# A fixed order on every engine for routed attention with a squared-ReLU feed-forward, its weights rounded as a pipeline

## The chip, the cores and the metric

The kernel runs on one core of a Trainium2 chip. A core has engines that run side by side, each with its own queue of instructions that it works off in order: TensorE (PE, matrix products; PEld is its loading of weights), VectorE (DVE), ScalarE (ACT), GpSimd (POOL) and SyncE (SP), which here issues the transfers between device memory and the core's memories. An engine waits for another by semaphores. SBUF is the working memory of 128 partitions; PSUM holds what TensorE writes, in eight banks. The metric is the device time of one execution in microseconds (us).

## The reference

Attention in which a query sees only the keys of its own cluster, and on its output a feed-forward block with a squared ReLU. All tensors are float32 (the weights come as float64 and are rounded on the chip).

```python
# q, k, v: (4, 8, 768, 64); centroids: (8, 16, 64)
q_assign = np.argmax(np.einsum('bhsd,hcd->bhsc', q_n, c_n), axis=-1)
k_assign = np.argmax(np.einsum('bhsd,hcd->bhsc', k_n, c_n), axis=-1)
mask = q_assign[:, :, :, None] == k_assign[:, :, None, :]
scores = np.where(mask, scale * np.matmul(q, k.transpose(0, 1, 3, 2)), -1e9)
attn = np.exp(scores - np.max(scores, axis=-1, keepdims=True))
x = np.matmul(attn / (np.sum(attn, axis=-1, keepdims=True) + 1e-9), v)
# x to (3072, 512); w_in: (512, 2048), w_out: (2048, 512)
r = np.maximum(x @ w_in, 0.0)
out = (r * r) @ w_out
```

## The kernel before

*Units.* Heads are worked on in pairs; a pair is two heads of one batch (`HP` = 4 pairs a batch, `NG` = 16 in all). A unit is one pair, one half `h` of the queries (384 of 768) and two of the six chunks of 128 keys. There are 96: first the four pairs of batch 0 with half 0 (units 0 to 11), then the same with half 1 (12 to 23), then each later pair with both halves. For each chunk, `scores` (L321) multiplies keys and queries of both heads into the PSUM tile `sc` and ACT takes the exponential into a tile `ex` (L337). For batch 0 the mask is a second product of one-hot cluster numbers on top of the scores (L332); for later pairs DVE multiplies `ex` by a comparison of cluster numbers (L339). POOL adds the six chunks up into `acc` (L347, L351). Two units later (`LAG`) `times_v` (L357) multiplies the exponentials by v into `av`. When a half is complete, `finish` sums `acc` over its partitions with a matmul into `sm` (L372), takes the reciprocal (L376), checks it (L378) and writes the quotient to `xT` (L382).

*Preparing a pair.* `prep` makes seven items for a pair: three `turn` (transposes of q and k into `pt`, copied to `qkT` by ACT, the second by DVE), `logits` (product with the centroids, copy `lgs`), `route` (transposes into `lt`, then four or five DVE steps that find the cluster, L258 to L279), and twice `turn_onehot` (batch 0) or `spread` (later pairs: two times three products `pb`, each three copied to `qid` by ACT). `load_qk(pair + 1)` is issued when a pair's transposes are done.

*Feed-forward.* `ffn(b, h)` is a generator of 112 steps for one half of a batch: 64 for `ph` (L395, four a tile, then ACT's ReLU L402 and DVE's square L403 into one of 16 `gT`), then 48 for `po` (L408), whose three results go by ACT to `osb` and out. `fill_steps` puts these steps among the units, evenly over those to come; what is left at the end runs alone.

*Banks.* Two banks each for `sc` and `av`; two (`ps_f`, by `bank`) for all else: `pt`, `lg`, `lt`, `po` of the one-hots, `pb`, `sm`, `ph`, `po`.

*Weights.* The 32 blocks of 128 x 512 float64 are read as pairs of words (`lo`, `hi`) and turned to float32 by `round_weights` (L118): DVE cuts out the exponent (L126), ACT shifts its bias (L129), DVE bounds it and sets the sign (L130, L134) and cuts out the mantissa (L139), ACT scales both halves (L142, L143), POOL adds them and multiplies (L144, L145, into `w_in` or `w_out`). Raw blocks have two buffers (`wstage`), `w_power` has one (`wtmp`). In the loop, 4/3 blocks are rounded in each of the first 12 units, two in each later one, until all 32 are done.

*Order.* The loop is traced unit by unit, and a scheduler then decides in which order the instructions stand on each engine; so TensorE's items of several steps can be taken apart and mixed.

Of the kernel before, what the change touches and what calls it, by code (L numbers as in the profile page):

```python
# [17 lines left out]
P = 128  # L18
# [5 lines left out]
def kernel(  # L24
# [27 lines left out]
    loads = ctx.enter_context(tc.tile_pool(name="loads", bufs=3))  # L52
# [8 lines left out]
    xtp = ctx.enter_context(tc.tile_pool(name="xtp", bufs=3))  # L61
    gtp = ctx.enter_context(tc.tile_pool(name="gtp", bufs=FT))
    outp = ctx.enter_context(tc.tile_pool(name="outp", bufs=1))
    wstage = ctx.enter_context(tc.tile_pool(name="wstage", bufs=2))
    wtmp = ctx.enter_context(tc.tile_pool(name="wtmp", bufs=1))
# [5 lines left out]
    def bank(name, shape):  # L71
        return ps_f.tile(shape, F32, name=name, tag="f")

# [38 lines left out]
    raw_w = {}  # L112

    def load_weights(i):
        raw_w[i] = wstage.tile([P, NW, 2], U32, name="w_raw")
        nc.sync.dma_start(raw_w[i], weights[i][1])

    def round_weights(i):  # L118
        dst = weights[i][0]
        w = raw_w.pop(i)  # L120
        lo, hi = w[:, :, 0], w[:, :, 1]
        lo_f, hi_f = lo.bitcast(F32), hi.bitcast(F32)
        power = wtmp.tile([P, NW], U32, name="w_power")
        power_f = power.bitcast(F32)

        nc.vector.tensor_scalar(  # L126
            out=power, in0=hi, scalar1=0x7FF00000, scalar2=None, op0=ALU.bitwise_and
        )
        nc.scalar.activation(out=power_f, in_=power, func=ACT.Relu, bias=rebias, scale=1.0)  # L129
        nc.vector.tensor_scalar(  # L130
            out=power, in0=power_f, scalar1=float(255 << 20), scalar2=8.0,
            op0=ALU.min, op1=ALU.mult,
        )
        nc.vector.scalar_tensor_tensor(  # L134
            out=power, in0=hi, scalar=0x80000000, in1=power,
            op0=ALU.bitwise_and, op1=ALU.bitwise_or,
        )

        nc.vector.tensor_scalar(  # L139
            out=hi, in0=hi, scalar1=0x000FFFFF, scalar2=None, op0=ALU.bitwise_and  # L140
        )
        nc.scalar.activation(out=hi_f, in_=hi, func=ACT.Copy, bias=1.0, scale=2.0 ** -20)  # L142
        nc.scalar.mul(out=lo_f, in_=lo, mul=2.0 ** -52)  # L143
        nc.gpsimd.tensor_tensor(out=hi_f, in0=hi_f, in1=lo_f, op=ALU.add)  # L144
        nc.gpsimd.tensor_tensor(out=dst, in0=hi_f, in1=power_f, op=ALU.mult)  # L145
# [5 lines left out]
    load_v(0)  # L151
# [11 lines left out]
    rebias = const.tile([P, 1], F32, name="rebias")  # L163
    nc.vector.memset(rebias, -float((1023 - 127) << 20))
# [10 lines left out]
    def centroids_norm():  # L175
# [6 lines left out]
        nc.scalar.sqrt(nrm, ss)  # L182
        for _ in range(2):
# [37 lines left out]
    def turn(pair, part):  # L221
# [7 lines left out]
        if part == 1:  # L229
            nc.vector.tensor_copy(out=dst, in_=pt)  # L230
        else:
            nc.scalar.copy(out=dst, in_=pt)
        if part == 2:
            raw.pop(pair)
            load_qk(pair + 1)
# [3 lines left out]
    def logits(pair):  # L239
# [8 lines left out]
        nc.scalar.copy(out=lgs[pair], in_=lg)  # L248

    def route(pair):  # L250
        lt = bank("lt", [P, NB, P])
        src = lgs.pop(pair)
        for i in range(NB):
            nc.tensor.transpose(out=lt[:, i], in_=src[:, i * P : (i + 1) * P], identity=ident)
        n = NB * P // C
# [8 lines left out]
        nc.vector.tensor_tensor(  # L264
# [16 lines left out]
    def turn_onehot(pair, which):  # L281
# [9 lines left out]
        if which == 0:  # L291
            nc.scalar.copy(out=dst, in_=src)
        else:
            nc.vector.tensor_scalar(
                out=dst, in0=src, scalar1=BIG, scalar2=-BIG, op0=ALU.mult, op1=ALU.add
            )

    def spread(pair, e):
        src, dst = qid[pair]
        for g in range(2):  # L300
# [6 lines left out]
            nc.scalar.copy(out=dst[:, g, e], in_=pb.rearrange("p i n -> p (i n)"))  # L307

# [12 lines left out]
    def scores(pair, h, c):  # L321
# [16 lines left out]
        for e in range(0 if pair < HP else 2):  # L338
            nc.vector.scalar_tensor_tensor(  # L339
                out=t[:, e], in0=qid[pair][1][:, h, e],  # L340
                scalar=ids[pair][:, c % NB, 2 + c // NB, e : e + 1], in1=t[:, e],
                op0=ALU.is_equal, op1=ALU.mult,
            )
        ex[pair, h, c] = t
        if c == 1:
            acc[pair, h] = accp.tile([P, 2, TB], F32, name="acc")
            nc.gpsimd.tensor_tensor(  # L347
                out=acc[pair, h], in0=ex[pair, h, 0], in1=t, op=ALU.add
            )
        elif c > 1:  # L350
            nc.gpsimd.tensor_tensor(out=acc[pair, h], in0=acc[pair, h], in1=t, op=ALU.add)  # L351

    def times_v(pair, h, c):
# [7 lines left out]
        if c > 0:  # L361
            ex.pop((pair, h, c))
            ex.pop((pair, h, 0), None)

    def finish(pair, h):
        b, hp = divmod(pair, HP)
        if hp == 0:
            xT[b, h] = xtp.tile([P, KT, TB], F32, name="xT")
        total = acc.pop((pair, h))
        sm = bank("sm", [P, TB])  # L370
        for e in range(2):
# [3 lines left out]
        rb = rbp.tile([P, TB], F32, name="rb")  # L375
        nc.vector.reciprocal(out=rb, in_=sm)  # L376
        ok = once.tile([P, TB], BF16, name="ok")
        nc.vector.scalar_tensor_tensor(  # L378
            out=ok, in0=rb, scalar=2.0 ** -100, in1=rb, op0=ALU.is_ge, op1=ALU.is_gt,
            accum_out=good[:, 2 * pair + h : 2 * pair + h + 1],  # L380
        )
        nc.vector.scalar_tensor_tensor(  # L382
            out=xT[b, h][:, hp], in0=av.pop((pair, h)), scalar=UP, in1=rb,
            op0=ALU.mult, op1=ALU.mult,
        )
# [4 lines left out]
    def ffn(b, h):  # L390
        gT = []
        for f in range(FT):
            ph = bank("ph", [P, TB])
            for kk in range(KT):
# [4 lines left out]
                if kk < KT - 1:  # L399
                    yield  # L400
            gT.append(gtp.tile([P, TB], F32, name="gT"))
            nc.scalar.activation(out=gT[f], in_=ph, func=ACT.Relu)  # L402
            nc.vector.tensor_tensor(out=gT[f], in0=gT[f], in1=gT[f], op=ALU.mult)  # L403
            yield
        for i in range(NB):
            po = bank("po", [P, DM])
            for f in range(FT):
# [4 lines left out]
                if f < FT - 1:  # L412
                    yield
# [3 lines left out]
            yield  # L417
# [9 lines left out]
    LAG = 2  # L427
    per_half = FT * KT + NB * FT
    fill = []
    left = [0]  # L430

    def fill_steps(n):
        while n > 0 and fill:
            if next(fill[0], "end") == "end":
                fill.pop(0)
            else:
                n -= 1
                left[0] -= 1

    def next_pair(u):  # L440

        pair, h, c = units[u]
        if c == 0 and pair + 1 < NG and h == 0 and (pair + 1) not in qkT:
            if pair + 1 < HP or pair >= HP:
                return pair + 1
# [4 lines left out]
    to_round = iter(range(len(weights)))  # L450
    loaded = iter(range(len(weights)))
    centroids_norm()
    for item in prep(0):
        item()
    ahead = []
    left_units = [0]
    rounding = 0.0
    for _ in range(2):
        load_weights(next(loaded))
    for u in range(len(units) + LAG):  # L460
        if u < len(units):
            pair, h, c = units[u]
            if (p := next_pair(u)) is not None:
                ahead.extend(prep(p))
            if c == 0 and pair not in raw_v:
                load_v(pair)
            for i in range(2):
                scores(pair, h, c + i)
        done = None
        if u >= LAG:  # L470
            pair, h, c = units[u - LAG]
            for i in range(2):
                times_v(pair, h, c + i)
            if c == NCH - 2:
                done = pair, h

        rounding += 4 / 3 if u < 12 else 2
        while rounding >= 1:
# [231 lines left out]
```

## Time and profile before

| | us |
|---|---|
| median of three runs | 1231.68 (1231.52 to 1233.67) |
| the profiled execution, its own time | 1233.24 |
| its span, first to last instruction | 1231.4 |
| PE busy | 1135.8 (92%) |
| DVE busy | 578.6 (47%) |
| POOL busy | 381.3 (31%) |
| ACT busy | 336.2 (27%) |

The page divides the span in 40 slices of 30.8 us and gives the busy share of each in tenths (9 is 90% or more), and the clock that TensorE was granted (PEclk, in tenths of full speed):

```profile
PE   6677776689999999999999999999999999999997
DVE  4466746441386865566445654266345653210110
ACT  4433343432233323232212231223212221110110
POOL 2655655442143433432232322233132332000000
PEclk7877798879999999999999999999999999999999
```

Busy time of a matmul is modelled and matmuls overlap, so a full PE isn't PE at its peak: what a matmul costs in a dense stretch is read from start to start.

### The profile page before, as it was taken

Reading aid. Unit: us, or ns where it says so; the run is one execution under the profiler, and the core shown is the slowest. Engines: PE = TensorE matmul, PEld = TensorE weight load, DVE = VectorE, ACT = ScalarE, POOL = GpSimd, SP = SyncE. Lnnn points to the kernel's source line nnn. Section 1 sums busy time; section 2 is a strip of 40 time slices with the busy share of each in tenths; the row PEclk is TensorE's granted clock in tenths of the full one; section 3 lists DMA queues with packets and bytes.
Section 4 is the critical chain, followed back from the end, with each engine's and each line's share of the span. In section 5 each row is a group of like instructions: output and inputs, shape, how many; then the busy total and the mean of one; then the engine's idle time right before and its main releaser. Section 6 shows DMA issues by size and latency. Waiting matters only on the chain.

```text
span 1231.4 us, 10628 instructions
## 1 busy us (share of the span) xinstructions
PE 1135.8 (92%) x4115; PEld 516.2 (42%) x4115; DVE 578.6 (47%) x795; ACT 336.2 (27%) x543; POOL 381.3 (31%) x233
## 2 busy tenths in 40 slices
PE   6677776689999999999999999999999999999997
PEld 3223232234444444444444444444444544554553
DVE  4466746441386865566445654266345653210110
ACT  4433343432233323232212231223212221110110
POOL 2655655442143433432232322233132332000000
PEclk7877798879999999999999999999999999999999
DMA  6332222211201101101001010201000000000000
GB/s 177 87 93 75 79 69 82 90 52 38 56 1 38 39 1 48 47 9 39 1 18 48 1 39 9 56 1 26 9 9 22 1 1 18 9 1 18 9 9 20
DMA packets 63881, 44.30 MB, mean 36 GB/s; under 512 B 51536, under 2 KB 56656, under 8 KB 63824
## 3 DMA queue, kind: packets, MB, share of 16 engines
q1 hardware_dynamic: 63824, 43.56, 12.4%
q8 instruction: 34, 0.56, 0.2%
q14 instruction: 23, 0.19, 0.0%
HBM read 37.26 MB, written 6.29 MB: 35 GB/s over the span
## 4 chain that ended last, share of the span: by engine, by line
PE 77%; POOL 8%; issue 8%; DVE 4%; ACT 2%; DMA 0%; SPq 0%; POOLq 0%; ACTq 0%
PE po L408 27%; PE ph L395 24%; PE sc L325 10%; PE av L357 9%; POOL acc L351 3%; POOL w_raw L144 2%; PE sm L372 2%; PE pt L227 2%; POOL w_out L145 1%; POOL w_in L145 1%; DVE w_power L126 1%; PE pb L303 1%; PE lg L243 1%; ACT ex L337 1%; DVE ids L269 0%
## 5 line engine op out<-in xcount | busy, mean ns | idle before, releaser
L395 PE MATMUL ph<-xT,w_in 128*128 128x384 f32 x1024 | 361.6, 502 | 27.4 <-ACT gT L402 26.3
L351 POOL TENSOR_TENSOR acc<-acc,ex 128x768 f32<-128x768 f32 x128 | 245.9, 1921 | 398.1 <-DVE ex L339 322.6
L408 PE MATMUL po<-w_out,gT 128*128 128x512 f32 x768 | 349.9, 602 | 0.0
L339 DVE SCALAR_TENSOR_TENSOR ex<-qid,ids,ex 128x384 f32<-128x384 bf16 x288 | 229.1, 847 | 157.9 <-ACT ex L337 157.7
L395 PEld LDWEIGHTS ph<-xT,w_in 128*128 128x128 f32 x1024 | 189.9, 193 | 186.9 <-issue 32.3
L408 PEld LDWEIGHTS po<-w_out,gT 128*128 128x128 f32 x768 | 140.5, 191 | 175.1 <-issue 170.6
L325 PE MATMUL sc<-qkT 64*128 64x384 f32 x768 | 195.0, 546 | 12.2 <-ACT ex L337 12.2
L337 ACT ACTIVATE ex<-sc 128x768 f32<-128x768 f32 x192 | 148.1, 806 | 197.0 <-PE sc L325 152.3
L403 DVE TENSOR_TENSOR gT<-gT 128x384 f32<-128x384 f32 x128 | 91.8, 721 | 177.7 <-ACT gT L402 177.4
L357 PE MATMUL av<-ex,v_raw 128*64 128x384 f32 x768 | 161.9, 521 | 0.0
L402 ACT ACTIVATE gT<-ph 128x384 f32<-128x384 f32 x128 | 62.5, 488 | 250.8 <-PE ph L395 250.8
L325 PEld LDWEIGHTS sc<-qkT 64*128 64x128 f32 x768 | 77.0, 197 | 105.1 <-issue 64.2
L376 DVE RECIPROCAL rb<-sm 128x384 f32<-128x384 f32 x32 | 81.7, 2554 | 80.6 <-PE sm L372 80.6
L347 POOL TENSOR_TENSOR acc<-ex 128x768 f32<-128x768 f32 x32 | 58.4, 1826 | 174.7 <-DVE ex L339 153.3
L357 PEld LDWEIGHTS av<-ex,v_raw 128*64 128x64 f32 x768 | 50.8, 141 | 93.3 <-issue 91.5
L126 DVE TENSOR_SCALAR w_power<-w_raw 128x512 uint32<-128x512 uint32 x32 | 32.6, 1020 | 78.0 <-POOL w_out L145 39.9
L415 ACT COPY osb<-po 128x512 f32<-128x512 f32 x24 | 14.0, 585 | 176.2 <-PE po L408 145.9
L144 POOL TENSOR_TENSOR w_raw<-w_raw 128x512 f32<-128x512 f32 x32 | 33.3, 1040 | 79.9 <-ACT w_raw L142 79.9
L129 ACT ACTIVATE w_power<-w_power,rebias 128x512 f32<-128x512 uint32 x32 | 23.1, 722 | 82.0 <-DVE w_power L126 82.0
L307 ACT CAST qid<-pb 128x384 bf16<-128x384 f32 x48 | 21.9, 480 | 40.2 <-PE pb L303 40.0
L142 ACT ACTIVATE w_raw<-w_raw 128x512 f32<-128x512 uint32 x32 | 21.4, 668 | 41.7 <-DVE w_raw L139 41.7
L372 PE MATMUL sm<-acc,ups 128*64 128x384 f32 x128 | 30.2, 536 | 2.7 <-ACT gT L402 2.7
(70 smaller groups left out, 423.2 us busy)
## 6 DMA issues: line engine op xcount, KB each, us to landing
w_raw<-in_moe_w_in_dram SPq DMA_DIRECT2D x16, 512.0 KB, 3.8
w_raw<-in_moe_w_out_dram SPq DMA_DIRECT2D x16, 512.0 KB, 3.5
v_raw<-in_v_dram SPq DMA_DIRECT2D x20, 384.0 KB, 3.2
q_raw<-in_q_dram SPq DMA_DIRECT2D x32, 192.0 KB, 3.6
k_raw<-in_k_dram SPq DMA_DIRECT2D x32, 192.0 KB, 3.2
out_dram<-osb SPq DMA_DIRECT2D x24, 256.0 KB, 2.0
cen<-in_centroids_dram SPq DMA_DIRECT2D x1, 32.0 KB, 1.7
```

The source lines that it names most:

```text
L144: nc.gpsimd.tensor_tensor(out=hi_f, in0=hi_f, in1=lo_f, op=ALU.add)
L325: nc.tensor.matmul(sc[:, e, 0:TB], lhsT=qkT[pair][rows, NCH + c], rhs=qkT[pair][rows, NB * h : NB * (h + 1)], start=True, stop=pair >= HP,)
L337: nc.scalar.activation(out=t, in_=sc[:, :, 0:TB], func=ACT.Exp, scale=SCALE)
L339: nc.vector.scalar_tensor_tensor(out=t[:, e], in0=qid[pair][1][:, h, e], scalar=ids[pair][:, c % NB, 2 + c // NB, e : e + 1], in1=t[:, e], ...
L347: nc.gpsimd.tensor_tensor(out=acc[pair, h], in0=ex[pair, h, 0], in1=t, op=ALU.add)
L351: nc.gpsimd.tensor_tensor(out=acc[pair, h], in0=acc[pair, h], in1=t, op=ALU.add)
L357: nc.tensor.matmul(av[pair, h][D * e : D * (e + 1)], lhsT=raw_v[pair][:, e, c], rhs=ex[pair, h, c][:, e], start=(c == 0), stop=(c == NCH - 1),
L376: nc.vector.reciprocal(out=rb, in_=sm)
L395: nc.tensor.matmul(ph, lhsT=w_in[:, kk, f * P : (f + 1) * P], rhs=xT[b, h][:, kk], start=(kk == 0), stop=(kk == KT - 1),)
L402: nc.scalar.activation(out=gT[f], in_=ph, func=ACT.Relu)
L403: nc.vector.tensor_tensor(out=gT[f], in0=gT[f], in1=gT[f], op=ALU.mult)
L408: nc.tensor.matmul(po, lhsT=gT[f][:, i * P : (i + 1) * P], rhs=w_out[:, f], start=(f == 0), stop=(f == FT - 1),)
```

## The change

The tracing loop now runs under `tc.manual_schedule()`: on each engine instructions stand in the order in which they are traced. To trace work of other engines where it is to stand, a clock counts TensorE's time: `tick(us)` moves it on with each piece of TensorE work, and `defer(us, what)` puts `what` off until that clock has gone so far.

- `times_v` follows one unit after the scores instead of two; masks, adds, squares and the division are put off by fixed times; `finish` stands between `times_v` and the fill, one unit later than `times_v` of its last chunks. Items of `prep` are three a unit (two from unit 24) with the fill between them; each item stays whole.
- Rounding is three deferred parts: `bits` (DVE, five steps; the bias is now DVE's too), `scale` (ACT, 3.5 us later) and `join` (POOL, 6.0 us later). A raw block and its `w_power` have six buffers up to block 19 (two in `wraw_l`, four in `wraw_r`); from block 20 on only the two of `wraw_l`, since the `gT` tiles take the room of `wraw_r`. Loads run four blocks ahead.
- `load_qk(pair + 2)` with four buffers instead of three; v is loaded three units ahead.
- The second `turn` copy of batch 0 and the second one-hot copy go from DVE to ACT; from pair 8 on one step of `route` goes from DVE to POOL. A first exponential of one column is traced at the start. The check of the sums is traced before the last 224 steps.

The diff, cut to its core (declarations of pools and arguments that say nothing new are left out):

```diff
-    loads = ctx.enter_context(tc.tile_pool(name="loads", bufs=3))
+    loads = ctx.enter_context(tc.tile_pool(name="loads", bufs=4))
...
+    wraw_l = early_l.enter_context(tc.tile_pool(name="wraw_l", bufs=2))
+    wraw_r = early_r.enter_context(tc.tile_pool(name="wraw_r", bufs=4, side="right"))
...
+    def defer(us, what):
+        clock[1] += 1
+        heapq.heappush(put_off, (clock[0] + us, clock[1], what))
+
+    def tick(us):
+        clock[0] += us
+        while put_off and put_off[0][0] <= clock[0]:
+            heapq.heappop(put_off)[2]()
...
     def load_weights(i):
-        raw_w[i] = wstage.tile([P, NW, 2], U32, name="w_raw")
-        nc.sync.dma_start(raw_w[i], weights[i][1])
+        pool = wraw_r if i < RIGHT and i % 3 else wraw_l
+        raw_w[i] = (
+            pool.tile([P, NW, 2], U32, name="w_raw"), pool.tile([P, NW], U32, name="w_power")
+        )
+        nc.sync.dma_start(raw_w[i][0], weights[i][1])
...
-        nc.scalar.activation(out=power_f, in_=power, func=ACT.Relu, bias=rebias, scale=1.0)
...
+        def bits():
...
+            nc.vector.tensor_scalar(
+                out=power_f, in0=power, scalar1=-float((1023 - 127) << 20), scalar2=0.0,
+                op0=ALU.add, op1=ALU.max,
+            )
...
+        def scale():
+            nc.scalar.mul(out=lo_f, in_=lo, mul=2.0 ** -52)
+            nc.scalar.activation(
+                out=hi_f, in_=hi, func=ACT.Copy, bias=1.0, scale=2.0 ** -20
+            )
+
+        def join():
+            nc.gpsimd.tensor_tensor(out=hi_f, in0=hi_f, in1=lo_f, op=ALU.add)
+            nc.gpsimd.tensor_tensor(out=dst, in0=hi_f, in1=power_f, op=ALU.mult)
+            raw_w.pop(i)
...
-        if part == 1:
+        if part == 1 and pair >= HP:
             nc.vector.tensor_copy(out=dst, in_=pt)
         else:
             nc.scalar.copy(out=dst, in_=pt)
+        tick(0.55)
         if part == 2:
             raw.pop(pair)
-            load_qk(pair + 1)
+            load_qk(pair + 2)
...
-        nc.vector.tensor_tensor(
+        (nc.gpsimd if pair >= 2 * HP else nc.vector).tensor_tensor(
...
+        odd = c % 2
+        if pair >= HP:
+            defer(1.9 + 0.3 * odd, mask)
+        defer((3.1 if pair >= HP else 1.8) + 1.0 * odd, add)
+        tick(0.75)
...
+        def divide():
+            rb = rbp.tile([P, TB], F32, name="rb")
+            nc.vector.reciprocal(out=rb, in_=sm)
...
+        defer(0.9, divide)
+        tick(0.75)
...
-            nc.vector.tensor_tensor(out=gT[f], in0=gT[f], in1=gT[f], op=ALU.mult)
-            yield
+            defer(0.9, lambda t=gT[f]: nc.vector.tensor_tensor(out=t, in0=t, in1=t, op=ALU.mult))
+            yield 0.65
...
+    def blocks():
+
+        for i in range(len(weights)):
+            if i == RIGHT:
+                early_r.close()
+                later["gT"] = ctx.enter_context(
+                    tc.tile_pool(name="gtp", bufs=FT, side="right", reuse_waits="tile")
+                )
+            bits, scale, join = round_weights(i)
+            bits()
+            defer(3.5, scale)
+            defer(6.0, join)
+            if i + AHEAD < len(weights):
+                load_weights(i + AHEAD)
+            yield
+
+    AHEAD = 4
...
+    with tc.manual_schedule():
...
+        for u in range(len(units) + 2):
+            finished = finishing.pop(0) if finishing and finishing[0][0] == u else None
+            if u < len(units):
...
+                for i in range(2):
+                    scores(pair, h, c + i)
+            if 1 <= u <= len(units):
+                pair, h, c = units[u - 1]
+                for i in range(2):
+                    times_v(pair, h, c + i)
+                if c == NCH - 2:
+                    finishing.append((u + 1, pair, h))
...
+            if finished:
+                _, pair, h = finished
+                finish(pair, h)
+            owed += 1.34 if u < 12 else 2
+            while owed >= 1:
+                owed -= 1
+                if next(rounding, "end") == "end" and early_l is not None:
...
+            share = -(-left[0] // max(1, left_units[0]))
+            left_units[0] -= 1
+            items = [ahead.pop(0) for _ in range(min(3 if u < 24 else 2, len(ahead)))]
+            parts = len(items) + 1
+            for i in range(parts):
+                fill_steps(share * (i + 1) // parts - share * i // parts)
+                if u < 12:
+                    tick(0.8)
+                if i < len(items):
+                    items[i][1]()
...
+        tick(20)
+        fill_steps(per_half)
+        check_sums()
+        fill_steps(per_half * 2)
+        tick(20)
```

## The prediction

> **What bounds the kernel now.** I read the busy time by stage first. Columns: stretch in us, its length, then busy us and number of instructions of PE, PEld, DVE, ACT and POOL, then the granted clock, the DMA share and GB/s.
>
> ```profile
> 0.00:272.00 272.00, 191.80 (x737) 83.71 (x737) 146.06 (x217) 111.98 (x174) 142.73 (x107) 0.81 0.31 90
> 272.00:1058.00 786.00, 778.29 (x2928) 347.44 (x2928) 410.92 (x541) 204.90 (x331) 238.55 (x126) 1.00 0.08 23
> 1058.00:1224.00 166.00, 165.66 (x452) 85.04 (x450) 21.61 (x38) 19.09 (x39) 0.00 (x0) 1.00 0.03 10
> ```
>
> From 272 us on TensorE is full (778.3 of 786, 165.7 of 166) at clock 1.00: nothing but less TensorE work, or fewer waits, shortens that. Before 272 it does 737 of 4115 instructions, at clock 0.81. So the gain lies in the first 272 us. What sets that stage is the weight rounding, as the rows of its last step and the waits on it show (min/median/max ns, first and last start; then us in total, times, longest).
>
> ```profile
> L145 POOL TENSOR_TENSOR w_in<-w_raw,w_power x16: 1288/1292/1492, 17.8 to 156.9; 128x512 f32<-128x512 f32 x16
> L145 POOL TENSOR_TENSOR w_out<-w_raw,w_power x16: 1288/1293/1488, 163.0 to 274.2; 128x512 f32<-128x512 f32 x16
> DVE w_power L126 <- POOL w_out L145: 39.9, 15, 5.5
> DVE w_power L126 <- POOL w_in L145: 34.7, 14, 4.2
> ACT w_power L129 <- DVE w_power L126: 82.0, 29, 4.8
> POOL w_raw L144 <- ACT w_raw L142: 79.9, 24, 13.9
> ```
>
> 32 blocks end between 17.8 and 274.2: 8.3 us a block. One w_power buffer makes a block's chain DVE, ACT, DVE, ACT, POOL, DVE serial: 0.43+0.72+0.43+0.69+0.43+0.67+1.04+1.29 = 5.7 us, and the rest is waiting. Where from, the timeline shows (start us, us, engine, line):
>
> ```profile
> 55.86 0.43 DVE L139 TENSOR_SCALAR w_raw<-w_raw 128x512 uint32<-128x512 uint32 x1
> ...
> 60.28 1.80 POOL L351 TENSOR_TENSOR acc<-acc,ex 128x768 f32<-128x768 f32 x1
> ...
> 60.36 2.01 DVE L126 TENSOR_SCALAR w_power<-w_raw 128x512 uint32<-128x512 uint32 x1 [4.07 <-POOL w_in L145]
> ...
> 68.12 3.75 POOL L351 TENSOR_TENSOR acc<-acc,ex 128x768 f32<-128x768 f32 x2
> ...
> 68.19 2.01 DVE L126 TENSOR_SCALAR w_power<-w_raw 128x512 uint32<-128x512 uint32 x1 [1.19 <-POOL w_in L145]
> ```
>
> The same DVE operation takes 0.43 us alone and 2.01 when a POOL add has just begun: it ends 0.29 after the add (62.37 against 62.08). In this stage 12 of 30 L126 and 7 of 30 L139 are held like that; reductions and copies out of PSUM never are. So DVE's rounding steps and POOL's work exclude each other, and this is what I price the change with.
>
> **The rounding, as a pipeline.** It takes the ACT step away (32 x 0.72 us, and one hop of the chain) and adds a DVE step, an add and max on 128x512, not in the trace; nearest rows are L130 (0.43) and, as the other end, L134 (0.69); I take 0.43, the one-input form. A block now costs DVE 4 x 0.43 + 0.69 = 2.4 us. With own buffers the chain no longer binds, but the exclusion does. The new order on POOL and DVE binds units and blocks together, so count to the start of unit 20, when all 32 blocks are rounded. POOL: 33 adds (5 per three units) x 1.80 + 32 x (1.04+1.29) = 134 us. DVE steps that can be held: 32 x 2.4 = 77; 14 squares L403 and 5 L378 x 0.55 = 10; 3 routes x 1.1 = 3; sum 90. Both: 224 us. A held step overlaps its holder by 0.43-0.29 = 0.14, and a held POOL step likewise by about that (L145: 1.29 becomes 1.49 behind 0.33 us of DVE). If all 185 DVE and 97 POOL steps were held, 37 us go: 187.
>
> The Trainium skill, "SBUF — State Buffer", section "Who interferes with whom", calls the pair of ports that DVE and GpSimd share an exclusive lock, whoever comes second fully blocked for the whole instruction. By that, nothing overlaps, unit 20 starts at 17+224 = 241 and the sum below gives 1249, slower than before; the row's 0.29 instead of 0.43 says a little does overlap.
>
> So unit 20 starts after 187 us (port never idle) to 224; and, as it is shared out before (133 POOL + 76 DVE = 209 of the 253 us from 19 to 272, 83%), it could take 187/0.83 = 225 on the overlapping count too. DVE's steps that are not held (reciprocals 5 x 2.55, reductions) run beside POOL, and six buffers give both a stock, so I take 195, near the low end. The count starts when the first block lands: ahead of it on SP now stand cen, q and k of three pairs and v, 2.75 MB, and itself 0.5; at the 216 GB/s of the first 15 us that is 15 + 1.2 of issue, 17 us (before: 12.5). Unit 20 at 17+195 = **212** (204 to 242).
>
> The six buffers serve 20 blocks; the last 12 alternate between two, so load i+2 waits for the join of i: 3.5 (landing) + 2.4 + 0.67 + 2.33 + hops 0.3 = 9.2 us a round of two. The exclusion alone makes such a unit 11.5 us (six units: 10 adds, 12 blocks, 14 squares: 69 us), so it is hidden; if held steps lengthen the round to 14 it costs 6 x 2.5 = 15. SP then stands at these loads with v behind it; v is wanted three units later, which covers it. ACT's scale steps stand ahead of exponentials and relus in its queue, so TensorE can't run far ahead of DVE.
>
> **What is left after unit 20.** Before does its work after 272 in 1223.5-272 = 951.5 us. After unit 20 the new order has more left: it has issued 112 of the 1024 ph matmuls against 133 (21 x 0.323 = 6.8), no po against 16 (x 0.429 = 6.9), 20 units of scores against 22.5 (2.5 x 1.49 = 3.7), 19 of av against 21 (2.4), and part of a pair's transposes (1): **+21**. Prices are the dense ones:
>
> ```profile
> 977.12 1.49 PE sc L325 x8
> ...
> 1058.24 41.63 PE ph L395 x128
> 1099.87 41.20 PE po L408 x96
> ```
>
> TensorE changes between kinds of work 578 times instead of 624, each about 0.1 us (416 against 323 ns between matmuls): **-4**.
>
> **New waits on TensorE.** In a fixed order it can't fill a wait with other work. Two banks (ps_f) serve everything but scores and av, and one is usually held by an open ph or po.
>
> ```profile
> 600.60 0.33 PE L303 MATMUL pb<-ident_b,ids_b 128*128 128x128 bf16 x3
> ...
> 600.77 1.08 PE L408 MATMUL po<-w_out,gT 128*128 128x512 f32 x2
> ...
> 600.97 0.48 ACT L307 CAST qid<-pb 128x384 bf16<-128x384 f32 x1 [0.35 <-PE pb L303]
> ```
>
> Here po ran while ACT emptied pb. Now the second three pb follow at once in the same bank: 601.45-600.60 less 0.17 of their own: 0.7 us, x 24 = 17. The first pb of a pair waits for the route: 0.31+0.56+0.56+0.60+0.55+0.16 plus a hop = 2.8 to 3.3 us after lt, against a third of a unit's fill, 1.1 to 2.6 us: about 1.0 x 12 = 12 (23 if masks stand ahead on DVE, or POOL, which from pair 8 does one of these steps in 0.6 to 1.04 us, is at an add). sm holds its bank until the reciprocal's end, 3.1 us later; now fill follows at once where scores did: nine places with less than that between, 7 in sum (5 to 21). ph in the bank just closed waits for the relu, 1.0 less 0.42, partly covered: 15 places, 6 in sum. Transposes 1. Sum 44 (42 to 69); before has some 12 of this kind after 272 (the 7.7 us idle of the window, and the part of each gap that modelled ends hide). Net **+32** (26 to 57).
>
> **Costed at nothing.** Loads of q and k two pairs ahead: no transpose waits for a DMA in the waits of before, 3.6 us to landing against units of 8 us or more. Four qkT copies (0.69) and four ohT (0.54) go from DVE to ACT, busy 27%: hidden; without that 5 us. The exponential's table load (1.28) moves ahead of the first exponential, under the start. The check of the sums moves ahead of the last matmuls: flag stood ready 0.3 us after them anyway. The tail of 7.9 us (copy 0.58, issue, landing 2.0, the flag's load 3.4) stays, 0 to -2.
>
> **Sum.** 212 + 951.5 + 21 - 4 + 32 + 7.9 = **1220** against this execution's span of 1231.4 (its time 1233.2; the median of the three runs 1231.7, so the span stands for it). It is even with before where unit 20 starts at 223, that is with the port 91% used.
>
> **Rivals.** (1) *Slower: the two engines still wait in turn.* DVE stands at a sum or a weight that is not there while POOL stands at a scale, and the port is used no better than before, 83%: 17+225 = 242, 1250; with the upper waits 1265. For it: the 83%, and in-order queues; against: six buffers. It decides from 223 on. (2) *Much faster: the rounding hardly meets POOL.* The holds of before are nearly all behind adds, few rows have a step beside a join (L264 once, held); if POOL alone sets the stage, 134 + 97 x 0.1 = 144, unit 20 at 161: 1169. Against: every L126 that met an add was held. (3) *Nothing:* start gain and bank waits cancel, 221 to 226 for unit 20, 1229 to 1234. (4) *It doesn't do what it says:* two buffers for the last 12 blocks bind them, +15: 1235; I count it with (1).
>
> **How the numbers follow.** 0.2% is 2.5 us, about what a measurement tells from no change. Forecast (1200 to 1229) 0.54; (2) 0.12; (3) 0.07; (1) with (4) 0.27. Faster 0.66, same 0.07, slower 0.27. The likeliest time is 1220, its own range 1200 to 1229. For 8 in 10: below, half of (2) is left out, 1185; above, the port at 83% with the lower waits, 1252.
>
> **What would show it.** L177's last start near 205 (not 250, not 160); the L149 to L165 rows of the rounding held to about 2 us in most cases, and POOL and held DVE steps together filling over nine tenths of 17 to 212; first ph near 140; TensorE over 97% busy after unit 20, with waits on pb of 0.7 us and on ids_b of about 1. Wrong if TensorE's windows after 300 us show far more idle than 5%, or if DVE steps run 0.43 us beside POOL.

## The result, and the profile after

The changed kernel takes 1283.7 us (median of four runs, 1282.87 to 1285.69), the kernel before 1232.3 in the same session: ratio 1.0418, 95% interval 1.0400 to 1.0436. It is slower by 4.2%; the forecast was 1220. Its profiled span is 1281.0, and all times below are spans from profiled executions, where not said otherwise; the ratios are of times against the kernel before, measured in the same session.

The busy time by stage, with the first two stretches of the prediction (start and end, length, busy us and number of PE, PEld, DVE, ACT, POOL, then the granted clock, DMA share, GB/s):

```profile
0.00:272.00 272.00, 182.53 (x832) 84.42 (x832) 207.84 (x250) 101.95 (x161) 157.00 (x111) 0.86 0.33 97
272.00:1058.00 786.00, 704.19 (x2689) 317.57 (x2687) 380.61 (x506) 193.48 (x313) 229.82 (x125) 0.97 0.07 20
1058.00:1274.00 216.00, 214.90 (x598) 105.34 (x595) 34.89 (x54) 24.95 (x46) 9.46 (x5) 1.00 0.03 10
```

The first stretch is better than before: TensorE issues 832 matmuls in it instead of 737. The second, which had been full (2928 matmuls, clock 1.00), now has 2689 at 704 of 786 us busy and clock 0.97. The time is lost there.

The rounding, by the row of its last step (ns, first and last start):

```profile
L177 POOL TENSOR_TENSOR w_in<-w_raw,w_power x16: 1289/1360/1617, 26.7 to 132.3; 128x512 f32<-128x512 f32 x16
L177 POOL TENSOR_TENSOR w_out<-w_raw,w_power x16: 1290/1352/1493, 141.0 to 226.7; 128x512 f32<-128x512 f32 x16
```

It ends at 228.0 instead of 275.5: the pipeline does its work. What stands in the way of it is what the prediction called the port, the exclusion between DVE's steps and POOL's work; a stretch of the timeline (start, length, engine):

```profile
215.14 3.94 POOL L390 TENSOR_TENSOR acc<-acc,ex 128x768 f32<-128x768 f32 x2
215.50 1.92 DVE L152 TENSOR_SCALAR w_power<-w_power 128x512 f32<-128x512 uint32 x1
...
217.46 1.91 DVE L156 TENSOR_SCALAR w_power<-w_power 128x512 uint32<-128x512 f32 x1
```

Two adds, two held steps of 1.9 us instead of 0.43. Of the 60 DVE steps in this stage (rounding, squares, checks of the sums, products of the route) that lay beside POOL's work for nine tenths of their length, 58 took longer than alone. Reciprocals aren't held: over the whole run 31 of 32 lay mostly beside POOL's work, and all took 2.54 to 2.56 us. From 27 to 228 us DVE is busy 185 of 201 us; with each step at its shortest it would be 109, so some two fifths of it is holding.

What TensorE waits for from unit 20 on (230 us; us in total, times, longest):

```profile
PE pb L340 <- DVE ids_b L317: 33.6, 12, 7.3
PE pt L262 <- DVE rb L429: 18.5, 8, 3.6
PE pb L340 <- ACT qid L344: 13.0, 23, 0.6
PE ph L450 <- ACT gT L457: 6.4, 11, 0.6
PE ph L450 <- DVE rb L429: 6.2, 4, 1.7
```

Before, from 272 to 1058 us, only two such rows stood there, 6.1 us on ids_b and 4.3 on a copy. In the first row TensorE stands for the route, which DVE works off in its own order:

```profile
311.14 3.76 DVE L380 SCALAR_TENSOR_TENSOR ex<-qid,ids,ex 128x384 f32<-128x384 bf16 x4 [7.58 <-ACT ex L375]
...
312.95 0.49 PE L291 MATMUL lt<-ident,lgs 128*128 128x128 f32 x3
313.28 1.46 PE L450 MATMUL ph<-xT,w_in 128*128 128x384 f32 x4
314.82 0.55 DVE L296 TENSOR_REDUCE mx<-lt 128x24 f32<-128x384 f32 x1
...
317.90 0.17 DVE L317 CAST ids_b<-ids 128x12 bf16<-128x12 f32 x1
```

The logits are turned (`lt`) at 313.4, but four masks keep DVE until 314.9; the route then takes 3.25 us, and TensorE has 1.3 us of fill. It is like this in four of the twelve pairs, where the route begins 1.2 to 1.4 us late; in six it is at most 0.4 late and the fill alone is too short; two are taken up below.

Why a sum holds its bank so long, and the transposes `pt` behind it stand, the timeline shows:

```profile
353.45 3.75 DVE L380 SCALAR_TENSOR_TENSOR ex<-qid,ids,ex 128x384 f32<-128x384 bf16 x4 [1.72 <-ACT ex L375]
354.43 0.82 PE L419 MATMUL sm<-acc,ups 128*64 128x384 f32 x4
354.77 2.02 POOL L390 TENSOR_TENSOR acc<-acc,ex 128x768 f32<-128x768 f32 x1 [4.77 <-DVE ex L380]
...
357.13 2.54 DVE L429 RECIPROCAL rb<-sm 128x384 f32<-128x384 f32 x1
...
359.73 1.09 PE L262 MATMUL pt<-ident,k_raw 128*128 128x128 f32 x4 [3.64 <-DVE rb L429]
```

The sum is ready at 355.2, but in DVE's order four masks stand ahead of the reciprocal, and one of them is held by a POOL add (3.75 us for four that take 2.2). So the reciprocal begins 1.9 us late and the bank is free 5.2 us after the sum began, not the 3.5 that was usual before. This holds for 23 of the 26 sums after unit 20.

The two longest waits have another cause (DVE, and TensorE's line behind it; "..." leaves out the steps between):

```profile
598.26 2.54 DVE L429 RECIPROCAL rb<-sm 128x384 f32<-128x384 f32 x1
613.09 0.56 DVE L430 SCALAR_TENSOR_TENSOR xT<-av,rb 128x384 f32<-128x384 f32 x1 [12.29 <-PE ph L450]
...
615.45 3.74 DVE L380 SCALAR_TENSOR_TENSOR ex<-qid,ids,ex 128x384 f32<-128x384 bf16 x4
619.11 0.55 DVE L296 TENSOR_REDUCE mx<-lt 128x24 f32<-128x384 f32 x1
...
622.65 0.17 DVE L317 CAST ids_b<-ids 128x12 bf16<-128x12 f32 x1
...
622.87 0.50 PE L340 MATMUL pb<-ident_b,ids_b 128*128 128x128 bf16 x3 [7.25 <-DVE ids_b L317]
```

DVE stood 12.3 us at the first write of an `xT` whose buffer the feed-forward of an older half still read; masks, route and `ids_b` queue behind, and TensorE stopped for 7.25 us at 615.6.

And a stop costs more than its length. The same four `ph` products, soon after a stop of 3.38 us and some 6 us later:

```profile
318.12 0.34 PE L340 MATMUL pb<-ident_b,ids_b 128*128 128x128 bf16 x3 [3.38 <-DVE ids_b L317]
...
319.30 2.87 PE L450 MATMUL ph<-xT,w_in 128*128 128x384 f32 x4
...
325.08 1.56 PE L450 MATMUL ph<-xT,w_in 128*128 128x384 f32 x4
```

2.87 against 1.56 us: around the end of the stop the granted clock goes to a half, for one to three of the clock's records of 3.41 us. From 230 us to the last matmul such records add up to some 58 us, before from 272 on to 7.

To have both in one ledger I priced each gap from one matmul's start to the next's at the usual gap of that pair of kinds and places in a group (30th percentile over both traces at full clock). What is over is put down to half clock as far as half-clock records cover the gap (at most half of the part covered, and at most the usual gap); of the rest, more than 0.2 us counts as a wait, less as work. The split is an estimate; the profile's own rows of waits after unit 20 add up to 84 us. In us, with before counted from its first matmul after 272 (at 273.6) and after from unit 20 at 230.2:

| | before | after | difference | predicted |
|---|---|---|---|---|
| TensorE's work | 924.1 | 927.5 | +3.4 | +21 - 4 |
| waits | 23.1 | 93.6 | +70.5 | +32 |
| half clock | 2.8 | 23.2 | +20.4 | 0 |
| after the last matmul | 7.9 | 6.5 | -1.4 | 0 |

### The profile page after: what moved, and what is told of

The parts are those of the page before. It is cut to its first block, busy times and chain, and to the rows that moved or that the text cites. A ratio compares the mean times of both kernels' runs of the same rounds, so it can differ in the third digit from the quotient of the medians.

```text
span 1281.0 us, 10655 instructions
## 1 busy us (share of the span) xinstructions
PE 1102.7 (86%) x4115; PEld 507.5 (40%) x4115; DVE 623.3 (49%) x810; ACT 321.0 (25%) x520; POOL 396.3 (31%) x241
## 4 chain that ended last, share of the span: by engine, by line
PE 66%; DVE 23%; ACT 4%; issue 3%; POOL 3%; DMA 1%; ACTq 0%; POOLq 0%; DVEq 0%
PE po L463 24%; PE ph L450 21%; PE sc L363 9%; DVE ex L380 8%; PE av L405 6%; DVE rb L429 4%; ACT ex L375 2%; DVE w_power L160 2%; PE pt L262 2%; DVE w_power L149 2%; DVE w_power L152 2%; DVE w_power L156 2%; POOL acc L390 1%; PE pb L340 1%; PE lg L279 1%
## 5 line engine op out<-in xcount | busy, mean ns | idle before, releaser
L450 PE MATMUL ph<-xT,w_in 128*128 128x384 f32 x1024 | 369.4, 506 | 48.1 <-DVE rb L429 22.2
L463 PE MATMUL po<-w_out,gT 128*128 128x512 f32 x768 | 359.2, 614 | 3.6 <-DVE rb L429 1.7
L363 PE MATMUL sc<-qkT 64*128 64x384 f32 x768 | 163.7, 536 | 11.0 <-ACT ex L375 11.0
L458 DVE TENSOR_TENSOR gT<-gT 128x384 f32<-128x384 f32 x128 | 78.6, 619 | 182.7 <-ACT gT L457 182.5
L405 PE MATMUL av<-ex,v_raw 128*64 128x384 f32 x768 | 146.3, 502 | 0.0
L363 PEld LDWEIGHTS sc<-qkT 64*128 64x128 f32 x768 | 69.3, 197 | 96.4 <-issue 61.8
L340 PE MATMUL pb<-ident_b,ids_b 128*128 128x128 bf16 x144 | 17.3, 236 | 46.6 <-DVE ids_b L317 33.6
L267 ACT COPY qkT<-pt 128x512 f32<-128x512 f32 x36 | 20.8, 586 | 89.0 <-PE pt L262 89.0
L160 DVE SCALAR_TENSOR_TENSOR w_power<-w_raw,w_power 128x512 uint32<-128x512 uint32 x32 | 41.2, 1287 | 1.1
L262 PE MATMUL pt<-ident,k_raw 128*128 128x128 f32 x96 | 18.4, 309 | 22.5 <-DVE rb L429 18.5
```

The costliest lines, as they stand in the source:

```text
L160: nc.vector.scalar_tensor_tensor(out=power, in0=hi, scalar=0x80000000, in1=power, op0=ALU.bitwise_and, op1=ALU.bitwise_or,)
L262: nc.tensor.transpose(out=pt[:, i], in_=raw[pair][which][:, c], identity=ident)
L363: nc.tensor.matmul(sc[:, e, 0:TB], lhsT=qkT[pair][rows, NCH + c], rhs=qkT[pair][rows, NB * h : NB * (h + 1)], start=True, stop=pair >= HP,)
L405: nc.tensor.matmul(av[pair, h][D * e : D * (e + 1)], lhsT=raw_v[pair][:, e, c], rhs=ex[pair, h, c][:, e], start=(c == 0), stop=(c == NCH - 1),
L450: nc.tensor.matmul(ph, lhsT=w_in[:, kk, f * P : (f + 1) * P], rhs=xT[b, h][:, kk], start=(kk == 0), stop=(kk == KT - 1),)
L458: defer(0.9, lambda t=gT[f]: nc.vector.tensor_tensor(out=t, in0=t, in1=t, op=ALU.mult))
```

## The experiments

The theory after the result: unit 20 starts 18 us later than predicted, in a stage that the port still binds; the rest is TensorE's stops in a fixed order, of three kinds (pb behind the route, anything behind a sum, the second pb behind a copy), and the half clock behind them. Each kind can be taken out alone by moving a few instructions in the order.

**e1_split.** Each group of three pb is an item of its own:

```diff
-    def spread(pair, e):
+    def spread(pair, e, gs=(0, 1)):
         src, dst = qid[pair]
-        for g in range(2):
+        for g in gs:
...
-        ] + [lambda i=i: (turn_onehot if pair < HP else spread)(pair, i) for i in range(2)]
+        ] + ([lambda i=i: turn_onehot(pair, i) for i in range(2)] if pair < HP else [
+            lambda e=e, g=g: spread(pair, e, [g]) for e in range(2) for g in range(2)
+        ])
...
+                    counts = [3, 3, 3] if p < HP else [3, 3, 3] if p == HP else [2, 2, 3, 2]
```

`counts` is how many of a pair's items each unit takes, so that they stay in their units, but for the second group of the first such pair.

> The changed kernel with its four pb groups of a pair as four items with fill matmuls between them; nothing else moves but one place in a unit. My theory: after unit 20 (from 230 us on) the changed kernel loses its time in waits of TensorE that a fixed order cannot fill; 16.9 us of them are the second group of three pb behind ScalarE's copy out of the same bank (23 times 0.57 and a little). These go; the first pb of a pair gets a quarter instead of a third of a unit's fill ahead of it, which costs about 4. 1281 - 17 + 4 = 1268 (1264 to 1273). Rival, the loss is not TensorE's but VectorE's or GpSimd's pace: the waits move elsewhere and the span stays at 1278 to 1284.

Measured 1277.6 (ratio to before 1.0372, 1.0355 to 1.0389): a miss. In the ledger the second-pb waits fell from 16.9 to 3.5 us as expected, but those of the first pb rose from 33.8 to 39.2, half clock from 23.2 to 25.9 (12 stops of 1.9 us and more instead of 10), work by 1.6, and unit 20 came 1.8 later. The first pb now has less fill ahead of it, while DVE gets to `ids_b` no sooner. The rival's range nearly holds the span, but the rows are not its rows.

**e2_route.** The first spread of a pair comes a unit after the route:

```diff
                     ahead.extend((p, item) for item in prep(p))
+                    counts = [3, 3, 3] if p < HP else [3, 2, 2] if p == HP else [2, 2, 1, 2]
...
-            items = [ahead.pop(0) for _ in range(min(3 if u < 24 else 2, len(ahead)))]
+            take = counts.pop(0) if counts else 0
+            items = [ahead.pop(0) for _ in range(min(take, len(ahead)))]
```

> The changed kernel with the route alone in its unit and both spreads a unit later (two items in units 1, 2 and 4 of a pair, one in unit 3). My theory: the 33 us in which TensorE stands at the first pb for ids_b (11 times, two of them 7.25 us) go nearly all, and with them the half-clock records that follow these stops (some 37 us of record, 18 us of time): 1281 - 31 - 18 = 1232 (1226 to 1246), mean granted clock from 0.947 to about 0.96. Rival 1, TensorE only catches up with VectorE and stops a unit later (at ex, rb or the qid copy): over 1265. Rival 2, the half clock does not come from the stops: 1248 to 1254 with the clock unchanged.

Measured 1227.8 (median time 1231.6, ratio 0.9991, 0.9982 to 1.0001), clock 0.963: as expected, 53 us from one item of each of twelve pairs put a unit later. The row of waits on `ids_b` is gone, the others stay:

```profile
PE pt L262 <- DVE rb L429: 18.5, 8, 3.6
PE pb L340 <- ACT qid L344: 10.2, 18, 0.6
PE ph L450 <- DVE rb L429: 6.2, 4, 1.7
```

In the ledger waits fell by 35 us and half clock by 16.5, though nothing was done to the clock.

**e3_finish.** The sums ahead of the unit's scores, for three pairs of a batch in four:

```diff
             finished = finishing.pop(0) if finishing and finishing[0][0] == u else None
+            early = finished and finished[1] % HP > 0
+            if early:
+                finish(*finished[1:])
...
-                finish(pair, h)
+                if not early:
+                    finish(pair, h)
```

> The changed kernel with the sums (and the reciprocal behind them) ahead of the unit's scores instead of behind its av, except for the first pair of a batch. My theory: sm's bank is held for 5 us because the reciprocal stands behind four masks on VectorE; ahead of the scores it is freed while scores and av run, so three quarters of the 26 us of waits on rb go and the half clock behind three of them (13.6 us of record, 6 of time): 1281 - 19 - 6 = 1256 (1250 to 1264). Rival: the masks now stand behind the reciprocal, so av or the route come late by up to 2.5 us in each of 24 units: 1281 to 1300.

Measured 1254.0 (ratio 1.0171, 1.0154 to 1.0188). As expected; the rows on `rb` after unit 20 fell from 27.3 to 10.1 us, and the masks, now behind the reciprocal, made no new wait there: the row on `ids_b` stayed at 33.6.

**e7_xt4.** A fourth buffer for `xT`:

```diff
-            pool = xtp if (2 * b + h) % 3 < 2 else later["xT"]
+            pool = xtp if (2 * b + h) % 4 < 2 else later["xT"]
...
-                        tc.tile_pool(name="xtp_late", bufs=1, reuse_waits="tile")
+                        tc.tile_pool(name="xtp_late", bufs=2, reuse_waits="tile")
```

> The changed kernel with four xT buffers in rotation instead of three, nothing else. In the changed kernel VectorE stands for 12.3 us at the first xT write of a half because the buffer's old half is still read by ph; masks and the route queue behind it, and the first pb comes 7.25 us late, in two places (the longest two of the 12). My theory: these two shrink to the 3.3 us of the others and their 17 us of half clock to about 7: 1281 - 8 - 5 = 1268 (1262 to 1274). Rival, the stand is covered since the route is late anyway: 1279 to 1283.

Measured 1264.8 (ratio 1.0258, 1.0241 to 1.0275), as expected: the waits of pb after a `po`, the two long ones among them, fell from 17.9 to 5.5 us in the ledger, half clock by 5.

**e4_all.** The four together, with all sums ahead of the scores (`counts` is 3, 2, 4 for the first pair with a spread and 2, 2, 1, 2, 2 for the others).

> The changed kernel with all three (pb groups apart, route apart, sums ahead of scores in every unit that has them) and with four xT buffers instead of three, so that VectorE does not stand for 12 us at the first write of an xT whose buffer is still read. My theory: 17 + 33 + 26 us of waits and about 20 us of the 23 us of half clock go: 1281 - 96 = 1185 (1180 to 1200), faster than the kernel before by 3 to 4%. Rival, VectorE or GpSimd set the pace behind these waits: 1225 to 1260.

Measured 1174.3 (median time 1175.1, ratio 0.9527, 0.9511 to 0.9543): 4.7% faster than the kernel before, and below the range expected. It had 96 us going; in the ledger 84 us of waits and all 23 of half clock went. The four alone gave 3 + 53 + 27 + 16 = 99 us, together 107. All waits of TensorE from unit 20 to the last matmul (its lines are two further on):

```profile
PE ph L452 <- ACT gT L459: 4.1, 11, 0.4
PE ph L452 <- DVE best L298: 1.5, 3, 0.7
PE po L465 <- DVE best L298: 0.7, 1, 0.7
PE ph L452 <- DVE flag L484: 0.2, 1, 0.2
```

And the middle stretch:

```profile
272.00:1058.00 786.00, 778.96 (x2967) 355.51 (x2966) 423.94 (x543) 204.68 (x335) 237.81 (x128) 1.00 0.08 21
```

2967 matmuls instead of 2689, clock 1.00 and not one half-clock record from unit 20 to the last matmul. So the fixed order as such isn't slow: from unit 20 to the last matmul it takes 941.8 us, with 9.8 of waits.

**e9_warm and e13_warm10.** Does the stop bring the half clock? Here TensorE works during the stop, on products that nothing reads (20, in e13_warm10 10), and all waits stay:

```diff
+    spare = [None]
...
     def spread(pair, e):
         src, dst = qid[pair]
+        if e == 0:
+            for _ in range(20):
+                nc.tensor.matmul(
+                    spare[0][:, 1, TB:512], lhsT=ident, rhs=ident, start=True, stop=True
+                )
...
         sc = ps_sc.tile([P, 2, 512], F32, name="sc")
+        spare[0] = sc
```

> The changed kernel with 20 small matmuls (128 columns, about 0.11 us each, 2.2 us in all) ahead of the first pb of every pair, into columns of the scores bank that nothing reads: TensorE works during the stop instead of standing, all waits stay. My theory: the stops themselves bring the half clock, so the records behind the pb stops (37 of the 63 us after unit 20) go and the granted clock rises from 0.947 to about 0.96, worth some 18 us; the 11 stops that are shorter than 2.2 us cost a few us more: 1281 - 18 + 3 = 1266 (1260 to 1272). Rival, the half clock has another cause (a period, the load of the chip): clock unchanged, 1281 to 1290.

> e9_warm with 10 instead of 20 small matmuls ahead of the first pb of a pair: in e9_warm each ran as two passes of 0.116 us, 4.6 us in all, longer than the stop that they fill. 10 take 2.3 us, shorter than 7 of the 12 stops. My theory: the half clock behind these stops goes as in e9_warm (there 11 us of time after unit 20 instead of 23), at some 4 us for the stops that are shorter: 1281 - 12 + 4 = 1273 (1268 to 1277), faster than the changed kernel though it does more. Rival, the filled stop is paid in full and the clock gains nothing: 1281 to 1285.

Measured 1293.9 (ratio 1.0507, 1.0489 to 1.0524) and 1278.3 (1.0368, 1.0351 to 1.0385). The place of the stop that was shown above, in e9_warm:

```profile
317.16 4.63 PE L341 MATMUL sc<-ident 128*128 128x128 f32 x40
321.63 0.33 PE L347 MATMUL pb<-ident_b,ids_b 128*128 128x128 bf16 x3
...
322.69 1.64 PE L458 MATMUL ph<-xT,w_in 128*128 128x384 f32 x4
```

The four `ph` behind it take 1.64 us instead of 2.87. The half clock after unit 20 fell from 23.2 to some 11 us in both, with the route and the sums as late as ever: the stops bring it. Both spans missed the expected range, though: in e9_warm 20 products took 4.63 us and not 2.2, which is more than its rival allowed too, and in e13_warm10 the filling cost some 7 us after unit 20 instead of 4, and unit 20 came 2 later. Still the median time fell from 1283.7 to 1278.8 (ratios 1.0418 and 1.0368, with intervals apart) for a kernel that has TensorE do 120 products more, each in two passes.

**e10_all_noadd and e11_all_onestep.** Is it the port that sets the start? Both are e4_all with work left out, on one side of the port each:

```diff
-            if c > 0:
+            if c == 1 or (c > 0 and pair >= HP):
                 nc.gpsimd.tensor_tensor(
```

> e4_all with four of five of GpSimd's adds of the first four pairs left out (the softmax sums of these pairs miss four chunks). About 27 of the adds before unit 20 go. My theory: up to unit 20 the port that VectorE's rounding steps and GpSimd share sets the time: 134 us of GpSimd and 95 of VectorE, 29 overlapping, 200 in all. 27 x 1.8 = 49 less, 8 of overlap lost: unit 20 starts at about 185 instead of 226: 1174 - 41 = 1133 (1126 to 1148). Rival 1, VectorE's own work and order set it: 1168 to 1178. Rival 2, something else (the loads, ScalarE, the one-hot) takes over halfway: 1148 to 1165.

> e4_all with four of the five VectorE steps of a block left out (only the first mask of bits stays; the weights are not the rounded ones). By the shared port: 32 x (3 x 0.43 + 0.69) = 63 us less on VectorE's side, 17 of overlap lost: unit 20 at about 180, 1174 - 46 = 1128 (1120 to 1145). If GpSimd alone set the stage (rival 2 of the prediction), it stays at 1165 to 1178. If VectorE alone set it: its 174 busy us of 205 fall by up to 125 us of held and unheld time, and the stage goes to where GpSimd or the loads bind, some 160: 1108.

Unit 20 started at 200.9 and 189.8 instead of 226.0, the spans were 1149.3 and 1138.2 (ratios 0.9318, 0.9302 to 0.9333, and 0.9224, 0.9208 to 0.9239). From unit 20 on both took 941.8 and 941.9 us, as in e4_all. So work taken from either engine shortens the stage, which a stage bound by POOL alone or by DVE alone wouldn't do. But it gave 25 and 36 us instead of 41 and 46; the span of e11_all_onestep lies in its range, that of e10_all_noadd in the range of its second rival, by which something else takes over halfway. In e4_all the two engines' sharing steps cover 94% of the time from 27 us to the last join, here 88%. What holds the other part then, these runs don't say.

**e8_all_relu.** The add-and-max step of blocks 0 to 19 back on ScalarE:

```diff
-            nc.vector.tensor_scalar(
-                out=power_f, in0=power, scalar1=-float((1023 - 127) << 20), scalar2=0.0,
-                op0=ALU.add, op1=ALU.max,
-            )
+            if i < RIGHT:
+                nc.scalar.activation(
+                    out=power_f, in_=power, func=ACT.Relu, bias=rebias, scale=1.0
+                )
+            else:
...
```

> e4_all with the add-and-max step of the first 20 blocks back on ScalarE as in the kernel before (0.72 us there instead of 0.43 on VectorE). By the shared port: 20 x 0.43 = 8.6 us less on VectorE's side, a few tenths of overlap lost each: unit 20 at 219 instead of 226, 1175 - 7 = 1168 (1164 to 1172). Rival, the chain from engine to engine sets the pace even with six buffers (two hops more a block, VectorE waits in order for ScalarE): 1178 to 1200.

Measured 1190.4 (ratio 0.9664, 0.9648 to 0.9680): the rival. DVE's waits from 20 to 240 us begin with

```profile
DVE w_power L161 <- ACT w_power L153: 44.2, 20, 5.6
```

DVE stands at each block for a step that stands in ScalarE's queue, and the port is covered to 85%. What the change brings by dropping the ScalarE step isn't the step's 0.72 us, but that DVE's five steps follow each other with no wait.

**e14_ahead.** The same, with the first step of the next block ahead of the rest of this one:

```diff
+                if i + 1 < RIGHT:
+                    steps[i + 1] = round_weights(i + 1)
+                    steps[i + 1][0]()
+                _, bits, scale, join = steps.pop(i)
                 bits()
```

> e8_all_relu with VectorE's first step of the next block, and with it ScalarE's add-and-max, ahead of the rest of this block (blocks 0 to 19), so that VectorE finds the ScalarE result ready. In e8_all_relu VectorE stood 20 times for it, 2.2 us each, 44 us, and VectorE and GpSimd together covered 85% of the stage instead of 94%. My theory: the stops go, the port's sum is 8.6 us less than in e4_all, and unit 20 starts at 219 to 222: 1175 - 6 = 1169 (1164 to 1174), a little faster than e4_all. Rival, ScalarE's queue (exponentials that wait for TensorE) is the pace and the result is late a block ahead too: 1178 to 1192.

Measured 1168.5 (median time 1170.9, ratio 0.9504, 0.9491 to 0.9518), unit 20 at 220.1: as expected, the waits fell from 44.2 to 10.2 us, and the cover rose to 94%. This is the fastest kernel here that leaves nothing out.

**e12_all_two.** Two rounding buffers for all blocks:

```diff
-    RIGHT = 20
+    RIGHT = 0
...
-    AHEAD = 4
+    AHEAD = 2
```

> e4_all with two rounding buffers for all 32 blocks (and loads two ahead) instead of six for the first 20: what the four more buffers bring. By the port the stage takes 6.5 us a block, 13 a round of two; a round of two buffers is 3.5 landing + 2.4 + 0.67 + 2.33 + 0.3 = 9.2 unheld and, with VectorE's steps held as in the trace (4.4 us a block more), about 14: just beyond it, 10 rounds x 1 = +10: 1185 (1178 to 1200). Rival 1, fully hidden: 1173 to 1177. Rival 2, in-order queues turn each missing block into stops of TensorE and half clock: over 1205.

Measured 1191.7 (ratio 0.9687, 0.9671 to 0.9703), unit 20 at 243.3 instead of 226.0: within the range, and more than its middle. DVE now waits 40.5 us for the loads of blocks, 0.7 in e4_all. So six buffers and loads four ahead are worth 17 us against two and two.

## Why the prediction was wrong

The step that failed is "New waits on TensorE": 32 us net where the ledger shows 70.5, and a cost that it didn't have at all, 20.4 us of half clock. That is 59 of the 61 us between 1220 and 1281. The later start (+18) is nearly cancelled by work and tail that were counted too high (-15) and by the 1.5 us that the ledger of before leaves out behind 272; that these cancel is luck. Within the 32, the waits themselves were put at 44 and measured 93.6, and those of before, which are taken off, at 12 and measured 23.1.

*The port and the start: right, some sizes off.* The prediction had 134 us of POOL and 90 of DVE to the end of the rounding; the trace has 133.8 and 90.4. It let 29 us overlap; measured, 24.7. The first block was read from 19.7 us, not 17. Some 9 us of idle in that stage were not in it, nor the 2.2 us between the rounding's end and unit 20. 212 became 230.2. The Trainium skill ("SBUF — State Buffer", section "Who interferes with whom") has whoever comes second of DVE and GpSimd fully blocked at their shared ports. By that nothing would overlap; the trace's 24.7 us are near the 29 that the prediction read from its row. That 230.2 lies nearer to the 241 of full exclusion than to 212 is luck, since neither sum has the idle time. The rival that the port would be used only 83% is false: DVE's sharing steps and POOL's work covered 95% of the stage, by the same count 80% in before. The rival of POOL alone is false too. One sign did not come: 68 of the 160 rounding steps were held, not most. e10_all_noadd and e11_all_onestep bear out the port as the main bound, not as the only one.

*Work after unit 20: 17 us predicted, 3.4 in the ledger.* Before had issued less by 272 us than the prediction read from the windows, where an instruction that crosses an edge stands twice: 128 ph, 22 units of scores and 20 of av, not 133, 22.5 and 21. After had issued 116 ph by unit 20 and no po, and has 449 changes of kind after it against 475. At the prediction's prices that gives 14 us. Where the other 11 us are wasn't tried.

*First pb of a pair: 12 us predicted, 33.6 measured.* The estimate took the route's DVE steps to follow the transposes at once, as they did in before (0.04 us in all twelve pairs), and named masks in the way only as an upper end of 23. Route against fill alone would still have come to about 14, near the 12. The other 19.5 us are the time by which the route began late: 13.4 in the two pairs behind the 12.3 us stand at `xT`, which the prediction did not have, 5.3 behind the masks of four pairs, under 1 elsewhere. Before has the same three `xT` buffers, and there the route never began late.

*Banks behind a sum: 7 us predicted (to 21), 27.3 measured* (rows on `rb`: 18.5, 6.2, 1.7, 0.9). It held the bank for 3.1 us; with the masks ahead it is 5.2. e3_finish took most of this away by moving the sum alone. The term for `ph` behind a relu, 6 us, was right: the row on `gT` has 6.4.

*Second pb: 17 predicted, 16.9 in the ledger.* The size was right, but taking it out alone was worth 3 us (e1_split) while the first pb still waits.

*Half clock: not in the sum.* The trace of before had a sign of it: a granted clock of 0.81 where TensorE had stops, 1.00 where it had none. The prediction had no term for it where it added new stops.

*Costed at nothing:* held for the loads two pairs ahead and the moved copies; no row on a transfer of q or k stands in TensorE's waits, and those on the `qkT` copies come to 3.4 us over the whole span. Rival (4), two buffers that bind the last 12 blocks, is false too: DVE waits 7.2 us in all for loads between 17 and 228 us, 3.3 of them for the first block.

*Two bounds that don't add up.* The 1265 of rival (1) should be 1275 by its own terms (57 us of waits for 32), and the 1252 with the lower waits 1244; neither reaches 1281.

Its own sign of failure, more than 5% idle after 300 us, was the one that came: TensorE is busy 704 of the 786 us from 272 on.

## What to carry to other kernels

When an order is fixed by hand, follow every engine's queue, not TensorE's alone: what stands ahead of a producer in its own queue adds to the wait, and here moving twelve items by a unit was worth 53 us. Count a stop of TensorE as its length plus the half clock behind it (here 94 us of waits came with 23 more), and take the stops out together: one of the four edits gave 3 us alone, and all four gave 107 where their single gains add up to 99. The changed kernel with slack in front of each consumer and a fourth `xT` buffer is 4.7% faster than the kernel before, without them 4.2% slower.

## What the runs showed of the hardware

Over 14 traces, from 250 us on, I set the idle time between a matmul's modelled end and the next one's start against half-clock records that begin during the stop or up to 4.5 us behind it: 49 of 52 stops of 1.9 us and more have one (24 of them during the stop), of 73 between 1.0 and 1.75 us four. Many of these stops recur from kernel to kernel. The Trainium skill ("TensorE: Matmul & The Clock Gate", section "Why this matters for your kernels") advises no gaps over about 3 us between bursts; here 9 of the 11 stops between 1.9 and 2.8 us already had a half-clock record. A stop of 7.25 us brought three records of 3.41 us, or two.

A DVE step held by a POOL add ends a little after it, and the two overlap by a little: over the rounding stage of the changed kernel 24.7 us of 224. A held step stands in the profile as busy: of the 185 us that DVE is busy in the 201 from 27 to 228 us, 109 are its steps at their shortest.
